# A planned instruction order with longer assumed latencies, four PSUM banks for first products, and three strided units in place of two

## Chip, cores and metric

The kernel runs on one core of a Trainium2 chip. The metric is device time in microseconds (us) for one launch, a median over runs.

## What is computed

Attention with 8 heads of 64 over 8 batches of 576 tokens. Four heads are local (a query sees the 32 tokens that end with it), four are strided (a query sees the earlier tokens with the same residue modulo 32). The result, 4608 tokens of 512 numbers, goes through an FF layer with a SoLU activation and a layer norm between its two weights.

```python
mask_local = (rel >= 0) & (rel < stride)
mask_strided = (rel >= 0) & (pos[None, :] % stride == pos[:, None] % stride)
...
attn = np.exp(scores)
attn = attn / (np.sum(attn, axis=-1, keepdims=True) + 1e-09)
...
h = x @ w_in
h_max = np.max(h, axis=-1, keepdims=True)
e = np.exp(h - h_max)
sm = e / (np.sum(e, axis=-1, keepdims=True) + 1e-09)
solu = h * sm
...
ln = (solu - mu) / np.sqrt(var + 1e-06) * g_ln
return (ln @ w_out).astype(np.float32)
```

## The kernel before

**Attention units.** A batch is cut into units: two strided ones of 6 and 5 blocks (a block is 3 residues of 18 tokens, 54 queries against 54 keys) and three local ones of 3 blocks (64 queries against 96 keys). A unit's steps are: scores into s_ps on PE (L341 adds the mask, L346 multiplies), max and subtraction on DVE (L352, L353), exp on ACT (L355), sum and reciprocal on DVE (L356, L360, L361), scaling on POOL (L364), a high half in fp16 on ACT (L370) and the low half on DVE (L371), a transpose by DMA from p to pt (L373), second products into x_ps on PE (L394), and high and low half of x on ACT (L410) and DVE (L411) into the rings xhi and xlo. x_ps has two banks: local units take them in turn, a strided unit takes both.

**FF tiles.** There are 36 tiles of 128 tokens. Tile n: first products in two halves of 12 matmuls each into h_ps (L452 to L454, a half is 512 columns, one bank), the max on DVE (L459) and its scaling (L460), exp on ACT (L461), u = h times e on DVE (L463), its square sum on ACT (L467), small steps on POOL (L471 to L487), c in a high half on ACT (L484) and a low half on DVE (L485), a transpose by DMA from c to ct (L488), second products into o_ps in two halves of 12 matmuls (L492 to L494), and a scaled copy with the store on ACT (L500, L501). h_ps has three banks, and tile n takes the pairs (0, 1), (0, 2), (1, 2) in turn. The last tile takes x_ps for its first products, and the last two tiles take s_ps for their second.

**Preparation.** Weights come as 64-bit numbers that are decoded on ACT and DVE, scaled, and split into fp16 halves; V is scaled and split for every batch (L301, L302) and copied to other partitions by DMA (L317: ve for local, vd for strided units). All loads, moves and transposes are issued by SP, in one queue; only the output's stores are issued by ACT.

**The order.** Nothing is issued where it is written: every step is added to a `Plan` with an engine, a duration, a key (its due time, in the same unit for all engines) and the buffers that it reads and writes. `Plan.order` is a list schedule: at each point it takes, of the steps that are ready on an engine, the one with the lowest key, and its model says when the steps behind it are ready. A transfer ends `DMA_LATENCY` after its queue time, and a step on another engine is ready `HOP` after the one that it needs. The order that comes out is the order in which each engine gets its instructions; the times of the model go nowhere. The keys are UK for units (one unit per 1.0 of time), TK for tiles (1.11 apart).

In the plan a bank of h_ps or x_ps is a buffer of its own, `("h", i)` and `("x", i)`. The tensors themselves are one tile each, and the waits of the built program are set by the framework from the order.

Of the kernel before, what the change touches and what calls it, by code (L numbers as in the profile page):

```python
# [25 lines left out]
KL = QL + STRIDE  # L26
# [3 lines left out]

RS = 3
QS = RS * NI
R0 = {0: 0, 6: STRIDE - 5 * RS}
RES = [*range(6 * RS), *range(STRIDE - 5 * RS, STRIDE)]
SP = len(RES) * NI

UNITS = [(1, 0, 6), (1, 6, 5), (0, 0, 3), (0, 3, 3), (0, 6, 3)]
NU = len(UNITS)
P_SCALE = 64.0
EPS_SM = 1e-9  # L40
# [5 lines left out]

UK = [-40.0, -39.5, -39.0, -8.0, -7.0, *(n - 6.0 for n in range(5, B * NU))]
TK = [1.11 * t + 1.0 for t in range(NT)]  # L50
G2LAG = 0.55
KX = 0.5
# [8 lines left out]
class Plan:  # L61
# [6 lines left out]
    def __init__(self):  # L70
        self.steps = []
# [68 lines left out]
def attn_solu_kernel(ctx: ExitStack, tc: tile.TileContext, qloc, qstr, kloc, kstr, vloc, vstr, w_in, w_out, g, masks, out):  # L140
    nc = tc.nc
    sb = ctx.enter_context(tc.tile_pool(name="sb", bufs=1))
    ps = ctx.enter_context(tc.tile_pool(name="ps", bufs=1, space=PSUM))


    NTB, NPB, NPT, NCB, NCT = 4, 3, 2, 2, 3

    def buf(name, shape, dtype=F32, n=1):
        return [sb.tile(shape, dtype, name=f"{name}{i}") for i in range(n)]


# [12 lines left out]

    (mask_sb,) = buf("mask", [P, 3, KL])
    (mk_loc,) = buf("mk_loc", [P, 2, 3, KL], BF16)
    (mk_str,) = buf("mk_str", [P, 6, QS], BF16)
    (unit_sb,) = buf("unit", [P, P], BF16)
    t_sb = buf("t", [P, 12 * QS], n=NTB)
    m_sb = buf("m", [P, 24], n=NTB + 1)  # L170
    p_sb = buf("p", [P, 12, P], F16, n=NPB)
    pt_sb = buf("pt", [P, 12, P], F16, n=NPT)
# [23 lines left out]
    (gs_sb,) = buf("gs", [P, 8])  # L196

    s_ps = ps.tile([P, 2, 512], F32, name="s_ps")
    h_ps = ps.tile([P, 3, 512], F32, name="h_ps")
    x_ps = ps.tile([P, 2, 512], F32, name="x_ps")  # L200
    o_ps = ps.tile([P, DM], F32, name="o_ps")

    plan = Plan()
    add = plan.add
# [7 lines left out]
    def masks_bf16():  # L212
        m = mask_sb
        nc.vector.tensor_copy(mk_loc[:, 0, 0:1], m[:, 0:1])
        nc.vector.tensor_copy(mk_loc[:, 0, 1:3], m[:, 1:2].broadcast_to([P, 2, KL]))
        nc.vector.tensor_copy(mk_loc[:, 1], m[:, 1:2].broadcast_to([P, 3, KL]))
        nc.vector.tensor_copy(mk_str, m[:, 2:3, 0:QS].broadcast_to([P, 6, QS]))

    def load_masks(key):
        add("sp", 0.6, lambda: nc.sync.dma_start(mask_sb, masks), key, w=["mask_raw"])  # L220
# [47 lines left out]
    def load_qk(b, half, key):  # L268
        w = 2 * (S, SP)[half]
        k0 = 0 if half else KPAD  # L270
# [45 lines left out]
        for i, (dur, dst, src) in enumerate(moves):  # L316
            add("sp", dur, lambda dst=dst, src=src: nc.sync.dma_start(dst, src), key, r=[("v", a, 0), ("v", a, 1)], w=[("v2", a, i)])  # L317

    plan_x = [0]


    def unit(n, key):
        b, j = divmod(n, NU)
        half, b0, nb = UNITS[j]
        nq, nk = (QL, KL) if half == 0 else (QS, QS)
        nx = 2 * nb
        t, m, pb, ptb = t_sb[n % NTB], m_sb[n % (NTB + 1)], p_sb[n % NPB], pt_sb[n % NPT]
# [23 lines left out]
        w = nx * nk / 960  # L351
# [19 lines left out]
        add("dve", w + 0.1, lambda: nc.vector.tensor_tensor(lo, tv, hi, op=ALU.subtract), key + 0.45, r=[T, PB], w=[PB], lock=True)  # L371
        nt = nx if half else 2 * nx
        add("sp", 0.16 * nt, lambda: nc.sync.dma_start_transpose(ptb[:, 0:nt], pb[:, 0:nt].rearrange("p a k -> p (a k)")), key + 0.5, r=[PB], w=[PT])  # L373
        xb = plan_x[0] % 2
        if half == 0:
            plan_x[0] += 1
        X = [("x", xb)] if half == 0 else [("x", 0), ("x", 1)]

        def pv():
            for pair in range(2):  # L380
                for i in range(nb):
                    blk, x = b0 + i, pair * nb + i
# [28 lines left out]
        add("dve", nx * nq / 960 + 0.15, lambda: nc.vector.tensor_tensor(dl, src, dh, op=ALU.subtract), key + KX, r=[*X, *((*x, "h") for x in ring)],  # L411
            w=[(*x, "l") for x in ring])


    def ff(n, key):

        banks, halves = (((0, 1), (0, 1)), ((0, 2), (1, 0)), ((1, 2), (0, 1)))[n % 3]
        hv, o, O = h_ps[:, banks[0] : banks[1] + 1 : banks[1] - banks[0]], o_ps, "o"
        HH = [("h", i) for i in banks]

        if n >= NT - 2:
            o, O = s_ps[:, n % 2], ("s", n % 2)
        if n == NT - 1:
            hv, HH = x_ps, [("x", i) for i in range(2)]
# [4 lines left out]
        ring += [("xs", b % 2, b0, a) for b in bs for b0 in R0 for a in "hl"]  # L429
# [26 lines left out]
        for i in halves:  # L456
# [11 lines left out]
            r=[U, (ST, "mean")], w=[E, (ST, "sq")])  # L468
# [8 lines left out]
        def norms():  # L477
# [8 lines left out]
            r=[U, (ST, "r"), (C, 0)], w=[(C, 1)], lock=True)  # L486
# [182 lines left out]
```

## Time and profile before

| | us |
|---|---|
| median of 3 runs | 612.12 |
| lowest and highest | 610.24, 617.36 |
| the profiled execution | 613.98 |
| its span, first to last instruction | 612.3 |
| PE, DVE, ACT, POOL busy in the span | 496.2, 368.5, 297.6, 153.7 |
| mean granted clock of TensorE | 0.946 |

The profile is of one execution. Busy times of engines overlap, so they don't add up to the span. A matmul's duration in the rows (0.38 us) is longer than the distance to the next one (0.22 us), since matmuls are pipelined. A wait names the instruction that waited, then the one that released it.

### The profile page before, as it was taken

To read this page: it belongs to the slowest core of one execution; us is meant where nothing else is said; L and a number is where in the kernel's file an instruction comes from. 1 tells how busy PE (TensorE), PEld (TensorE's weight loads), DVE (VectorE), ACT (ScalarE), POOL (GpSimd) and SP (SyncE) were. 2 spreads that over 40 slices of the span, in tenths; PEclk is the share of its full clock that TensorE was granted. 3 is DMA by queue.
4 is the path that set the end of the run, shared out by engine and by line. 5 is a ranking of instruction groups with operands and counts; after the bars stand their busy time and mean duration, and the time that the engine had idled before them with its cause. 6 is when DMAs were issued, how large, how long until landed. Compare 5 with 4: busy or idle time off the path is not lost.

```text
span 612.3 us, 11764 instructions
## 1 busy us (share of the span) xinstructions
PE 496.2 (81%) x4808; PEld 254.8 (42%) x4808; DVE 368.5 (60%) x647; ACT 297.6 (49%) x437; POOL 153.7 (25%) x305
## 2 busy tenths in 40 slices
PE   0236925879987899899998999789998889899865
PEld 0233523435444454435454444434454444344322
DVE  3578888866567557666574667476665664333340
ACT  3746536545643565346543464356534453333440
POOL 2020004333222323223322132244222232113130
PEclk9999965989989999879998899799999998999979
DMA  8799587789529983988378847974497554422252
GB/s 320 292 241 280 149 155 206 179 179 233 99 55 205 247 216 78 204 212 201 79 164 199 212 95 171 216 194 114 100 211 125 108 97 82 85 53 52 51 112 59
DMA packets 171157, 96.89 MB, mean 158 GB/s; under 512 B 138208, under 2 KB 157280, under 8 KB 171104
## 3 DMA queue, kind: packets, MB, share of 16 engines
q1 hardware_dynamic: 165920, 86.71, 63.1%
q10 hardware_dynamic: 5184, 9.44, 4.9%
q8 instruction: 37, 0.61, 0.4%
q14 instruction: 16, 0.13, 0.1%
HBM read 39.24 MB, written 9.44 MB: 80 GB/s over the span
## 4 chain that ended last, share of the span: by engine, by line
PE 36%; DVE 23%; ACT 13%; DMA 12%; POOL 8%; issue 7%; ACTq 1%; SPq 0%; DVEq 0%; POOLq 0%
PE h_ps L452 7%; PE h_ps L454 6%; PE h_ps L453 6%; DVE u L463 4%; DMA pt<-p 4%; DVE st L459 4%; PE o_ps L492 4%; ACT e L461 4%; PE o_ps L494 4%; PE o_ps L493 4%; DMA ct<-c 3%; DMA vrl<-vloc 3%; POOL t L364 3%; DVE c L485 2%; PE x_ps L394 2%
## 5 line engine op out<-in xcount | busy, mean ns | idle before, releaser
L452 PE MATMUL h_ps<-w,xhi 128*128 128x512 f16 x280 | 112.5, 402 | 30.3 <-DVE st L459 14.3
L492 PE MATMUL o_ps<-obuf,ct 128*128 128x512 f16 x272 | 104.2, 383 | 11.4 <-DMA ct<-c 11.4
L453 PE MATMUL h_ps<-w,xhi 128*128 128x512 f16 x280 | 112.6, 402 | 0.0
L454 PE MATMUL h_ps<-w,xlo 128*128 128x512 f16 x280 | 112.4, 401 | 0.0
L493 PE MATMUL o_ps<-obuf,ct 128*128 128x512 f16 x272 | 104.0, 382 | 0.0
L494 PE MATMUL o_ps<-obuf,ct 128*128 128x512 f16 x272 | 103.9, 382 | 0.0
L461 ACT ACTIVATE e<-h_ps,st,vsc 128x1024 f32<-128x1024 f32 x31 | 37.3, 1204 | 109.5 <-PE h_ps L454 57.8
L471 POOL TENSOR_SCALAR st<-st 128x1 f32<-128x1 f32 x36 | 10.3, 286 | 293.1 <-DVE st L466 287.7
L364 POOL TENSOR_TENSOR t<-t,m 128x576 f32<-128x576 f32 (+2 forms) x40 | 52.5, 1314 | 122.6 <-DVE m L361 95.9
L463 DVE SCALAR_TENSOR_TENSOR u<-h_ps,e 128x1024 f32<-128x1024 f32 x35 | 42.8, 1222 | 64.0 <-ACT e L461 49.8
L485 DVE SCALAR_TENSOR_TENSOR c<-u,st,c 128x1024 f16<-128x1024 f32 x36 | 47.3, 1315 | 39.9 <-ACT c L484 39.9
L459 DVE TENSOR_REDUCE st<-h_ps 128x1 f32<-128x1024 f32 x35 | 42.5, 1216 | 32.2 <-PE h_ps L454 32.2
L467 ACT ACTIVATE e<-u,st 128x1024 f32<-128x1024 f32 x36 | 41.3, 1147 | 40.8 <-DVE st L466 40.8
L453 PEld LDWEIGHTS <-xhi 128*128 128x128 f16 x288 | 29.3, 102 | 63.1 <-issue 37.4
L484 ACT ACTIVATE c<-u,st 128x1024 f16<-128x1024 f32 x36 | 41.2, 1146 | 26.2 <-POOL st L481 25.3
L492 PEld LDWEIGHTS <-ct 128*128 128x128 f16 x288 | 28.4, 99 | 51.9 <-DMA ct<-c 19.2
L371 DVE TENSOR_TENSOR p<-t,p 128x576 f16<-128x576 f32 (+2 forms) x40 | 30.5, 762 | 26.1 <-ACT p L370 25.8
L454 PEld LDWEIGHTS <-xlo 128*128 128x128 f16 x288 | 29.5, 102 | 38.0 <-issue 7.1
L452 PEld LDWEIGHTS <-xhi 128*128 128x128 f16 x288 | 29.6, 103 | 35.2 <-issue 6.7
L494 PEld LDWEIGHTS <-ct 128*128 128x128 f16 x288 | 28.4, 99 | 34.6 <-issue 1.1
L346 PE MATMUL s_ps<-k,q 64*54 64x54 f32 (+1 forms) x1280 | 41.9, 275 | 0.0
L493 PEld LDWEIGHTS <-ct 128*128 128x128 f16 x288 | 28.4, 98 | 32.0 <-issue 0.8
(125 smaller groups left out, 730.0 us busy)
## 6 DMA issues: line engine op xcount, KB each, us to landing
out<-ob ACTq DMA_DIRECT2D x36, 256.0 KB, 3.4
vrs<-vstr SPq DMA_DIRECT2D x8, 768.0 KB, 6.9
vd<-vs SPq DMA_DIRECT2D x16, 384.0 KB, 5.9
vrl<-vloc SPq DMA_DIRECT2D x8, 640.0 KB, 6.2
q<-qstr SPq DMA_DIRECT2D x8, 594.0 KB, 4.9
k<-kstr SPq DMA_DIRECT2D x8, 594.0 KB, 6.0
q<-qloc SPq DMA_DIRECT2D x8, 576.0 KB, 6.2
k<-kloc SPq DMA_DIRECT2D x8, 576.0 KB, 5.9
```

The costliest lines, as they stand in the source:

```text
L346: nc.tensor.matmul(s_ps[row : row + nq, pair, i * nk : (i + 1) * nk], q_raw[half][hs, q0 : q0 + (nq - 1) * nqb + 1 : nqb], k_raw[half][hs, ...
L364: add("pool", nx * nk / 500 + 0.1, lambda: nc.gpsimd.tensor_tensor(tv, tv, sm.unsqueeze(2).broadcast_to([P, nx, nk]), op=ALU.mult), key + ...
L452: nc.tensor.matmul(hv[:, i], xhi[:, cc, tok], whi[:, cc, cols], start=(cc == 0), stop=False)
L453: nc.tensor.matmul(hv[:, i], xhi[:, cc, tok], wlo[:, cc, cols], start=False, stop=False)
L454: nc.tensor.matmul(hv[:, i], xlo[:, cc, tok], whi[:, cc, cols], start=False, stop=(cc == 3))
L459: add("dve", 1.21, lambda: nc.vector.tensor_reduce(nm, hv, axis=AX.XY, op=ALU.max, negate=True), key + 0.2, r=HH, w=[(ST, "nm")])
L461: add("act", 1.3, lambda: nc.scalar.activation(ev, hv, AF.Exp, bias=nm, scale=hs, accum_out=z), key + 0.25, r=[*HH, (ST, "nm"), *SC], w=[E ...
L463: add("dve", 1.3, lambda: nc.vector.scalar_tensor_tensor(uv, hv, 1.0, ev, op0=ALU.mult, op1=ALU.mult, accum_out=us), key + 0.3, r=[*HH, E] ...
L485: add("dve", 1.35, lambda: nc.vector.scalar_tensor_tensor(c[:, 1], u, r, c[:, 0], op0=ALU.mult, op1=ALU.subtract), key + 0.45, r=[U, (ST, ...
L492: nc.tensor.matmul(o, ct[:, cc, :], ohi[:, cc, :], start=(cc == 0), stop=False)
L493: nc.tensor.matmul(o, ct[:, cc, :], olo[:, cc, :], start=False, stop=False)
L494: nc.tensor.matmul(o, ct[:, 8 + cc, :], ohi[:, cc, :], start=False, stop=(cc == 7))
```

## The change

It changes the cost model of the plan, the sizes of the strided units, and the use of PSUM.

- `DMA_LATENCY` goes from 2.0 to 6.0 and `HOP` from 0.1 to 0.6.
- The strided half of a batch becomes three units of 4, 4 and 3 blocks. The second of them holds residues 12 to 17 and again 17 to 22 (residue 17 is computed twice, as before), so its copies into xhi and xlo are two instructions each. UK is stretched so that a batch takes the same time in keys.
- h_ps gets four banks, tile n takes the pair 0, 1 or 2, 3 in turn, the last tile too. x_ps has one bank, which every unit takes.

```diff
-UNITS = [(1, 0, 6), (1, 6, 5), (0, 0, 3), (0, 3, 3), (0, 6, 3)]
+NBS = SP // QS
+
+UNITS = [(1, 0, 4), (1, 4, 4), (1, 8, 3), (0, 0, 3), (0, 3, 3), (0, 6, 3)]
...
-UK = [-40.0, -39.5, -39.0, -8.0, -7.0, *(n - 6.0 for n in range(5, B * NU))]
+UK = [-40.0, -39.7, -39.4, -39.0, -8.0, -7.0, *(5 / 6 * n - 6.0 for n in range(NU, B * NU))]
...
-    DMA_LATENCY = 2.0
+    DMA_LATENCY = 6.0
     DMA_AHEAD = 1.0
-    HOP = 0.1
+    HOP = 0.6
...
-    h_ps = ps.tile([P, 3, 512], F32, name="h_ps")
-    x_ps = ps.tile([P, 2, 512], F32, name="x_ps")
+    h_ps = ps.tile([P, 4, 512], F32, name="h_ps")
+    x_ps = ps.tile([P, 512], F32, name="x_ps")
...
-        X = [("x", xb)] if half == 0 else [("x", 0), ("x", 1)]
+        X = ["x"]
...
+            res = RES[RS * b0 : RS * (b0 + nb)]
+            cuts = [0, *(i for i in range(1, len(res)) if res[i] != res[i - 1] + 1), len(res)]
+            parts = [(src[:, :, :, i:j], *(x[:, :, :, res[i] : res[i] + j - i] for x in to)) for i, j in zip(cuts, cuts[1:])]
...
-        banks, halves = (((0, 1), (0, 1)), ((0, 2), (1, 0)), ((1, 2), (0, 1)))[n % 3]
-        hv, o, O = h_ps[:, banks[0] : banks[1] + 1 : banks[1] - banks[0]], o_ps, "o"
-        HH = [("h", i) for i in banks]
+        h0 = n % 2 * 2
+        hv, o, O = h_ps[:, h0 : h0 + 2], o_ps, "o"
+        HH = [("h", h0 + i) for i in range(2)]
...
-        if n == NT - 1:
-            hv, HH = x_ps, [("x", i) for i in range(2)]
...
-        for j in range(2):
+        for j in range(3):
             unit(b * NU + j, UK[b * NU + j])
```

The order of every engine moves with it, and the line numbers of the unit's and the tile's steps by two to three. Three places follow; the numbers in the names are buffers and tell tiles and units apart.

SP in batch 2, from the transpose of the second strided unit's p on, before. ct1 and ct2 are the transposed c of tiles 4 and 5, pt0 holds the first local unit, vd is V for the strided units of batch 3:

```order
L373 DMA_TRANSPOSE pt1_101<-p2_99 128x10x128
L373 DMA_TRANSPOSE pt0_100<-p0_97 128x12x128
L488 DMA_TRANSPOSE ct1_111<-c0_108 128x16x128
L317 DMA vd0_77<-vs0_75 64x12x256 x2
L488 DMA_TRANSPOSE ct2_112<-c1_109 128x16x128
L271 DMA q00_63<-qloc 128x1152
L272 DMA k00_65<-kloc 128x1152
L373 DMA_TRANSPOSE pt1_101<-p1_98 128x12x128
L317 DMA vd0_77<-vs0_75 64x6x256 x2
```

and now, from the transpose of the third strided unit's p on:

```order
L371 DMA_TRANSPOSE pt0_100<-p2_99 128x6x128
L490 DMA_TRANSPOSE ct1_111<-c0_108 128x16x128
L371 DMA_TRANSPOSE pt1_101<-p0_97 128x12x128
L490 DMA_TRANSPOSE ct2_112<-c1_109 128x16x128
L271 DMA q00_63<-qloc 128x1152
L272 DMA k00_65<-kloc 128x1152
L317 DMA vd0_77<-vs0_75 64x12x256 x2
L317 DMA vd0_77<-vs0_75 64x6x256 x2
L371 DMA_TRANSPOSE pt0_100<-p1_98 128x12x128
```

The moves of vd, which wait for the split of V, stood between the two tiles' transposes and behind the next unit's, and now stand together behind the loads.

DVE from the max of tile 11 to its u, before (L459 max, L460 scaling, L463 u; L352, L353 and L371 belong to units, L411 is the low half of x):

```order
L459 TENSOR_REDUCE st3_118<-h_ps_130 128x1
L460 TENSOR_SCALAR st3_118<-st3_118,vsc2_82 128x1
L352 TENSOR_REDUCE m0_92<-s_ps_129 128x12
L411 TENSOR_TENSOR xlo0_103<-x_ps_131,xhi0_102 128x2x192
L371 TENSOR_TENSOR p1_98<-t3_91,p1_98 128x6x96
L353 TENSOR_TENSOR t0_88<-s_ps_129,m0_92 128x648
L463 SCALAR_TENSOR_TENSOR u1_107,st3_118<-h_ps_130,e1_105 128x1024
```

and now, between the same three of tile 11 (now L461, L462 and L465; the other lines have moved by two or three as well):

```order
L461 TENSOR_REDUCE st3_118<-h_ps_130 128x1
L302 SCALAR_TENSOR_TENSOR vs0_75<-vrs0_73,vsc0_80,vs0_75 128x1536
L350 TENSOR_REDUCE m3_95<-s_ps_129 128x6
L369 TENSOR_TENSOR p1_98<-t2_90,p1_98 128x6x96
L351 TENSOR_TENSOR t3_91<-s_ps_129,m3_95 128x576
L487 SCALAR_TENSOR_TENSOR c0_108<-u0_106,st2_117,c0_108 128x1024
L462 TENSOR_SCALAR st3_118<-st3_118,vsc2_82 128x1
L414 TENSOR_TENSOR xlo0_103<-x_ps_131,xhi0_102 128x2x192
L354 TENSOR_REDUCE m3_95<-t3_91 128x6
L358 TENSOR_SCALAR m3_95<-m3_95 128x6
L359 RECIPROCAL m3_95<-m3_95 128x6
L465 SCALAR_TENSOR_TENSOR u1_107,st3_118<-h_ps_130,e1_105 128x1024
```

The scaling, which exp needs, stood right behind the max and now stands behind the split of V, three steps of units and the low half of tile 10's c.

ACT over the last tiles, before (L461 exp, L467 square sum, L484 c, L500 the scaled copy of the second products; st0 to st3 are tiles 32 to 35):

```order
L461 ACTIVATE e1_105,st1_116<-h_ps_130,st1_116,vsc3_83 128x1024
L467 ACTIVATE e1_105,st1_116<-u1_107,st1_116 128x1024
L461 ACTIVATE e1_105,st3_118<-x_ps_131,st3_118,vsc3_83 128x1024
L484 ACTIVATE c1_109<-u1_107,st1_116 128x1024
L500 ACTIVATE ob0_113<-o_ps_132,st0_115 128x512
L501 DMA out<-ob0_113 128x512
L461 ACTIVATE e0_104,st2_117<-h_ps_130,st2_117,vsc3_83 128x1024
L467 ACTIVATE e1_105,st3_118<-u1_107,st3_118 128x1024
L467 ACTIVATE e0_104,st2_117<-u0_106,st2_117 128x1024
L484 ACTIVATE c1_109<-u1_107,st3_118 128x1024
L484 ACTIVATE c0_108<-u0_106,st2_117 128x1024
L500 ACTIVATE ob1_114<-o_ps_132,st1_116 128x512
```

and now:

```order
L463 ACTIVATE e1_105,st1_116<-h_ps_130,st1_116,vsc3_83 128x1024
L469 ACTIVATE e1_105,st1_116<-u1_107,st1_116 128x1024
L463 ACTIVATE e0_104,st2_117<-h_ps_130,st2_117,vsc3_83 128x1024
L502 ACTIVATE ob1_114<-o_ps_132,st3_118 128x512
L503 DMA out<-ob1_114 128x512
L486 ACTIVATE c1_109<-u1_107,st1_116 128x1024
L469 ACTIVATE e0_104,st2_117<-u0_106,st2_117 128x1024
L486 ACTIVATE c0_108<-u0_106,st2_117 128x1024
L463 ACTIVATE e1_105,st3_118<-h_ps_130,st3_118,vsc3_83 128x1024
L502 ACTIVATE ob0_113<-o_ps_132,st0_115 128x512
L503 DMA out<-ob0_113 128x512
L469 ACTIVATE e1_105,st3_118<-u1_107,st3_118 128x1024
```

Tile 35 stood ahead of tile 34, with x_ps for its first products; now the tiles stand in turn, and the scaled copy of tile 32's second products comes behind the exp of tile 35 instead of ahead of tile 34's. On PE the second products of tiles 32 to 35 now stand behind the last first product.

## Rows read from the trace of the kernel before

**Rows 1.** The page: the engines' line of part 1 and the chain of part 4.

```profile
PE 496.2 (81%) x4808; PEld 254.8 (42%) x4808; DVE 368.5 (60%) x647; ACT 297.6 (49%) x437; POOL 153.7 (25%) x305
...
PE 36%; DVE 23%; ACT 13%; DMA 12%; POOL 8%; issue 7%; ACTq 1%; SPq 0%; DVEq 0%; POOLq 0%
```

**Rows 2.** Three stretches: length, busy us by engine, then PEclk, DMA share, GB/s.

```profile
0.00:100.00 100.00, 40.62 (x604) 28.19 (x608) 73.32 (x142) 52.28 (x85) 13.19 (x20) 0.91 0.87 246
100.00:580.00 480.00, 436.22 (x4136) 218.98 (x4129) 287.32 (x495) 236.46 (x341) 134.53 (x271) 0.96 0.67 145
580.00:612.00 32.00, 19.40 (x78) 7.65 (x75) 7.88 (x11) 8.84 (x13) 5.96 (x14) 0.88 0.35 82
```

**Rows 3.** Waits of PE from 100 to 580 us: total us, times, longest.

```profile
PE h_ps L452 <- DVE st L459: 14.3, 13, 2.6
PE h_ps L452 <- DVE u L463: 9.0, 9, 1.4
PE x_ps L394 <- DMA pt<-p: 7.4, 7, 2.5
PE h_ps L452 <- ACT e L461: 6.7, 4, 1.8
PE o_ps L492 <- DMA ct<-c: 6.3, 6, 2.3
```

**Rows 4.** Waits of PE: the longest before 100 us, and those behind 580 us.

```profile
PE s_ps L341 <- DVE t L353: 21.6, 7, 5.2
...
PE o_ps L492 <- DMA ct<-c: 5.0, 1, 5.0
PE s_ps L492 <- DMA ct<-c: 2.8, 2, 1.5
```

**Rows 5.** Timeline, 176 to 200 us: tile 6's reads and tile 7's first half.

```profile
184.90 1.21 DVE L459 TENSOR_REDUCE st<-h_ps 128x1 f32<-128x1024 f32 x1
...
186.16 0.38 PE L452 MATMUL h_ps<-w,xhi 128*128 128x512 f16 x1 [1.91 <-DVE st L459]
...
188.95 1.21 ACT L461 ACTIVATE e<-h_ps,st,vsc 128x1024 f32<-128x1024 f32 x1 [6.16 <-PE h_ps L454]
...
190.28 1.22 DVE L463 SCALAR_TENSOR_TENSOR u<-h_ps,e 128x1024 f32<-128x1024 f32 x1 [2.46 <-ACT e L461]
```

**Rows 6.** Waits of ACT (first row) and of DVE from 100 to 580 us.

```profile
ACT e L461 <- PE h_ps L454: 57.8, 13, 7.9
...
DVE u L463 <- ACT e L461: 48.4, 22, 4.8
DVE st L459 <- PE h_ps L454: 32.2, 13, 3.9
```

**Rows 7.** The transposed tiles pt (first row) and ct: from issue to landing.

```profile
DMA to landing us min/median/max: 3.4/4.3/8.6
...
DMA to landing us min/median/max: 4.2/5.0/8.4
```

**Rows 8.** Timeline, 570 to 612 us: tile 33's max and its second products.

```profile
572.03 1.23 DVE L459 TENSOR_REDUCE st<-h_ps 128x1 f32<-128x1024 f32 x1 [3.30 <-PE h_ps L454]
...
586.17 0.61 PE L492 MATMUL o_ps<-obuf,ct 128*128 128x512 f16 x1 [5.04 <-DMA ct<-c]
```

**Rows 9.** Groups of instructions by line and shape: count, busy us, mean ns, idle before.

```profile
L353 DVE TENSOR_TENSOR t<-s_ps,m 128x648 f32<-128x648 f32 x8 | 6.6, 828 | 0.2
...
L353 DVE TENSOR_TENSOR t<-s_ps,m 128x540 f32<-128x540 f32 x8 | 5.8, 719 | 0.2
...
L361 DVE RECIPROCAL m<-m 128x10 f32<-128x10 f32 x8 | 1.7, 217 | 0.3
```

**Rows 10.** Timeline of PE, 200 to 270 us: the scores of one strided unit.

```profile
214.30 0.31 PE L341 MATMUL s_ps<-mk_str,unit 64*64 64x270 bf16 x4
214.44 1.15 PE L346 MATMUL s_ps<-k,q 64*54 64x54 f32 x40
```

More of the change, by code (lines that the diff above doesn't have):

```diff
@@ L32 @@
 QS = RS * NI
-R0 = {0: 0, 6: STRIDE - 5 * RS}
 RES = [*range(6 * RS), *range(STRIDE - 5 * RS, STRIDE)]
 SP = len(RES) * NI
-UNITS = [(1, 0, 6), (1, 6, 5), (0, 0, 3), (0, 3, 3), (0, 6, 3)]
+NBS = SP // QS
+UNITS = [(1, 0, 4), (1, 4, 4), (1, 8, 3), (0, 0, 3), (0, 3, 3), (0, 6, 3)]
 NU = len(UNITS)
@@ L166, in attn_solu_kernel @@
     (mk_loc,) = buf("mk_loc", [P, 2, 3, KL], BF16)
-    (mk_str,) = buf("mk_str", [P, 6, QS], BF16)
+    (mk_str,) = buf("mk_str", [P, 4, QS], BF16)
     (unit_sb,) = buf("unit", [P, P], BF16)
-    t_sb = buf("t", [P, 12 * QS], n=NTB)
+    t_sb = buf("t", [P, 6 * KL], n=NTB)
     m_sb = buf("m", [P, 24], n=NTB + 1)
@@ L216, in masks_bf16 @@
         nc.vector.tensor_copy(mk_loc[:, 1], m[:, 1:2].broadcast_to([P, 3, KL]))
-        nc.vector.tensor_copy(mk_str, m[:, 2:3, 0:QS].broadcast_to([P, 6, QS]))
+        nc.vector.tensor_copy(mk_str, m[:, 2:3, 0:QS].broadcast_to([P, 4, QS]))
     def load_masks(key):
@@ L317, in v_split @@
             add("sp", dur, lambda dst=dst, src=src: nc.sync.dma_start(dst, src), key, r=[("v", a, 0), ("v", a, 1)], w=[("v2", a, i)])
-    plan_x = [0]
     def unit(n, key):
@@ L373, in unit @@
         add("sp", 0.16 * nt, lambda: nc.sync.dma_start_transpose(ptb[:, 0:nt], pb[:, 0:nt].rearrange("p a k -> p (a k)")), key + 0.5, r=[PB], w=[PT])
-        xb = plan_x[0] % 2
-        if half == 0:
-            plan_x[0] += 1
-        X = [("x", xb)] if half == 0 else [("x", 0), ("x", 1)]
+        X = ["x"]
         def pv():
@@ L382, in pv @@
                     blk, x = b0 + i, pair * nb + i
+                    x_out = x_ps[:, x * nq :]
                     if half == 0:
-                        x_out = x_ps[:, xb, x * nq :]
                         vv, vb = (v_sb[0] if blk % 2 else ve_sb), (blk + 1) // 2
@@ L387, in pv @@
                     else:
-                        x_out = x_ps[:, pair, i * nq :]
                         vv, vb = vd_sb.rearrange("p a c y d -> p a (c y d)"), blk
@@ L401, in unit @@
             q0, w = off + QL * b0, QL * nb
-            src = x_ps[:, xb, 0 : 2 * w].rearrange("p (c q) -> p c q", c=2)
-            dh, dl = (x[:, 0:2, q0 : q0 + w] for x in (xhi, xlo))
+            src = x_ps[:, 0 : 2 * w].rearrange("p (c q) -> p c q", c=2)
+            parts = [(src, *(x[:, 0:2, q0 : q0 + w] for x in (xhi, xlo)))]
             ring = [("xl", q0 // QL + i) for i in range(nb)]
         else:
-            src = x_ps[:, :, 0 : nb * QS].rearrange("p c (r i) -> p c i r", i=NI)
-            dh, dl = (x[:, 2:4, off : off + S].rearrange("p c (i r) -> p c i r", r=STRIDE)[:, :, :, R0[b0] : R0[b0] + RS * nb] for x in (xhi, xlo))
@@ L409, in unit @@
-            ring = [("xs", b % 2, b0)]
-        add("act", nx * nq / 1200 + 0.17, lambda: nc.scalar.copy(dh, src), key + KX, r=X, w=[(*x, "h") for x in ring])
-        add("dve", nx * nq / 960 + 0.15, lambda: nc.vector.tensor_tensor(dl, src, dh, op=ALU.subtract), key + KX, r=[*X, *((*x, "h") for x in ring)],
-            w=[(*x, "l") for x in ring])
+            src = x_ps[:, 0 : nx * QS].rearrange("p (c r i) -> p c i r", c=2, i=NI)
+            to = [x[:, 2:4, off : off + S].rearrange("p c (i r) -> p c i r", r=STRIDE) for x in (xhi, xlo)]
@@ new lines, in unit, with x_hi, x_lo @@
+            res = RES[RS * b0 : RS * (b0 + nb)]
+            cuts = [0, *(i for i in range(1, len(res)) if res[i] != res[i - 1] + 1), len(res)]
+            parts = [(src[:, :, :, i:j], *(x[:, :, :, res[i] : res[i] + j - i] for x in to)) for i, j in zip(cuts, cuts[1:])]
+            ring = [("xs", b % 2, b0)]
+        def x_hi():
+            for src, dh, _ in parts:
+                nc.scalar.copy(dh, src)
+        def x_lo():
+            for src, dh, dl in parts:
+                nc.vector.tensor_tensor(dl, src, dh, op=ALU.subtract)
@@ L415, in ff @@
+        add("act", nx * nq / 1200 + 0.17 * len(parts), x_hi, key + KX, r=X, w=[(*x, "h") for x in ring])
+        add("dve", nx * nq / 960 + 0.15 * len(parts), x_lo, key + KX, r=[*X, *((*x, "h") for x in ring)], w=[(*x, "l") for x in ring])
     def ff(n, key):
-        banks, halves = (((0, 1), (0, 1)), ((0, 2), (1, 0)), ((1, 2), (0, 1)))[n % 3]
-        hv, o, O = h_ps[:, banks[0] : banks[1] + 1 : banks[1] - banks[0]], o_ps, "o"
-        HH = [("h", i) for i in banks]
+        h0 = n % 2 * 2
@@ L428, in ff @@
         ring = [("xl", pos // QL + i, a) for i in range(2) for a in "hl"]
-        ring += [("xs", b % 2, b0, a) for b in bs for b0 in R0 for a in "hl"]
+        ring += [("xs", b % 2, b0, a) for b in bs for half, b0, _ in UNITS if half for a in "hl"]
         e, u, c, ct, ob, st = e_sb[n % 2], u_sb[n % 2], c_sb[n % NCB], ct_sb[n % NCT], ob_sb[n % 2], st_sb[n % 4]
@@ L454, in g1 @@
                 nc.tensor.matmul(hv[:, i], xlo[:, cc, tok], whi[:, cc, cols], start=False, stop=(cc == 3))
-        for i in halves:
+        for i in range(2):
             add("pe", 2.6, lambda i=i: g1(i), key, r=[*ring, *(("w", cc) for cc in range(4))], w=[HH[i]])
@@ L594, in attn_solu_kernel @@
         v_split(b, 0, VK[b] + 2.5)
-        for j in range(2, NU - 1):
+        for j in range(3, NU - 1):
             unit(b * NU + j, UK[b * NU + j])
```

## The prediction

> **What bounds the kernel now.** I read the page's engine line and its chain first [rows 1]: TensorE (PE) is busy 81% of the span, but holds only 36% of the chain that ended last; VectorE (DVE), ScalarE (ACT), the transfers and POOL hold 23, 13, 12 and 8%. So PE has the most work, and still spends time waiting for a chain through the others. Then the stretches [rows 2]: in the first 100 us PE works 40.6 us, from 100 to 580 it works 436.2 of 480, in the last 32 it works 19.4. The middle is the run of token tiles; its idle time is 43.8 us.
>
> PE's waits in that middle [rows 3] add up to the same: 14.3 + 9.0 + 6.7 + 7.4 + 6.3 = 43.7. Of this 30.0 us stands before first products (L452), which wait for a read of h_ps; 7.4 before the attention's second products, which wait for a transposed p; 6.3 before the second products of the FF (L492), which wait for a transposed c. In the last stretch it is 5.0 + 2.8 us for c, and at the start the score matmuls wait 21.6 us for L353, the last DVE read of the scores [rows 4].
>
> The 30.0 us is not what the plan meant. In [rows 5] stand tile 6 (banks 0 and 1) and tile 7 (first half in bank 2). The first half of tile 7 (PE at 186.16) starts when the max of tile 6 (DVE at 184.90) has ended, 1.91 us late, though that max reads other banks. The exp of tile 6 (ACT at 188.95) has its max since 186.1, and starts only when that half has been written. In all, exp waited 57.8 us for first products and max 32.2 [rows 6]; how much of that is a tile's own products, the sums don't tell. I read it so: a write of h_ps and a read of h_ps exclude each other, in the order in which the steps are issued, whatever the bank.
>
> **The change, part by part.** The sum is made on the profiled execution: 613.98 us, of which 612.3 are its span; the median of the runs shown is 612.12, or 1.9 lower.
>
> *Transfers planned 6.0 instead of 2.0 us late.* With its own costs the plan before expects a p of 12 blocks after 0.55 + 1.92 + 2.0 = 4.5 us, and a c after 0.55 + 2.55 + 2.0 = 5.1. The trace has medians of 4.3 and 5.0, and largest ones of 8.6 and 8.4 [rows 7]. The new plan expects 8.5 and 9.1, the upper ends. An order holds no clock times, so a pessimistic plan costs PE nothing while other work stands in front of the late step; it puts more there. Between the scores of the first local unit of batch 2 and its second products PE had 5 half-steps of the FF (2.6 us each), now 8; between tile 5's last first product and its second products 6, now 9. On the SP queue, shown with the change, the vd moves no longer stand between two transposes of c. Of the 7.4 + 6.3 us I take 12; bounds 0 (what was late for one step is late for the next) and 13.7.
>
> The Trainium skill, "DMA: Bandwidth & Descriptors", section "Anatomy of one DMA — SWDGE (gpsimd) path", gives a DMA a fixed cost of about 2 us, on another issuing path than this. By it the old figure was right and this part would save nothing; the trace agrees at the median and not at the largest, and the largest are what PE waits for.
>
> *Hand-overs at 0.6 instead of 0.1 us, and four banks.* If reads and writes of h_ps still exclude each other, four banks free nothing by themselves. I went through both orders half by half and set the reads that stand ahead of a half (max 1.21, exp 1.21, u 1.22 [rows 5], and some 0.2 us behind each) against the PE work that stands there. From tile 4 to 33 that leaves 10 us of unavoidable wait before, and 10.5 now. The measured 30.0 is three times that, because the reads begin late: DVE waited 48.4 us for exp [rows 6]. A plan with longer hand-overs puts other work into such holes, so that later reads come sooner. But it also parts the reads of one tile: over tiles 4 to 30 there are 36 steps between a max and its scaling, where there were 9, and 78 between scaling and u, where there were 53; the DVE rows of tile 11, shown with the change, are the worst of it. I take -5 us; bounds -30 (all gone) and +30 (doubled).
>
> *The end.* Before, the last tile was started early, into x_ps, and its second products stood among those of the two tiles before, so PE met c three times with nothing else to do: 5.0 + 2.8 us. Now the order is plain, and the second products of tiles 32, 33 and 34, six half-steps or 15.5 us, stand between the last first product and tile 35's. Before, it took 14.1 us from the start of a max (572.03) to the second products that its c released (586.17) [rows 8]; this is now covered. New are two waits for h_ps: the max of tile 33 (1.2) and exp and u of tile 34 (2.7). Gain 7.8 - 3.9 = 3.9; bounds 0 and 7.8. The granted clock of this stretch is 0.88 [rows 2], so 12% of 32 us, 3.8, went to the lower level (1.2 GHz) after idle stretches; of this I count 2.
>
> *The clock in the run.* From 100 to 580 the mean granted clock is 0.96 [rows 2]: 19 us went to work at 1.2 GHz instead of 2.4. With some 40% of the run's idle time gone (17 of 43.8) I take 4 us; bounds 0 and 12.
>
> *Units of 4, 4 and 3 blocks.* The elements stay the same, the passes grow. From 828 against 719 ns at 648 and 540 elements [rows 9] the fixed part of a DVE pass is 828 - 648 x 109/108 = 174 ns; five such passes, the reciprocal's 0.22 and as much for the scaling ahead of it, and one more x_lo because the middle unit is cut in two: 0.87 + 0.44 + 0.17, some 1.4 us per batch. In the run DVE is busy 287 of 480 us [rows 2], which hides it; with that cover gone it would be 8 x 1.4 = 11 us. In the first 100 us DVE is waited for, and two batches stand there: +2.8. The extra mask matmuls cost PE 0.14 us (214.30 to 214.44) per unit [rows 10]: +1.1 for 8. ACT and POOL get a pass more on engines that are busy half the time; nothing.
>
> *One bank for x.* No second product waits for a read of x [rows 3]; in the built program each already waited for the last x_lo issued before, of either bank. So nothing in the run, and +1.1 at the start, where the first two strided units stand back to back on PE. The reads of the first tiles' h_ps stand closer there too: +1.9, by the same count as above. Bounds for both together 0 and 8.
>
> Sum: -12 - 5 - 3.9 - 2 - 4 + 2.8 + 1.1 + 1.1 + 1.9 = -20.0. From 613.98 that is 594.0, from the median 592.1. I say 593.
>
> **The rivals.**
> A, the pairs of banks part after all, and reads no longer hold the next tile's products. For it speaks the code, two pairs that never touch; against it [rows 5], where different banks did not help. Then another 20 of the 30.0 us and 8 of the clock go: 593 - 28 = 565.
>
> The Trainium skill, "PSUM — Partial Sum Buffer", section "Terms", forbids two engines only the same bank and quadrant at once; by that rule rival A is what the chip allows. The trace shows that this program orders more than that.
>
> B, no change: what the transfers no longer hold, the reads of h_ps do, since PE comes to them earlier. Then the -12, -5 and -4 fall away: 593 + 21 = 614, by the median's measure 613. For it: h_ps has 69% of the run's idle time.
>
> C, slower: the parted reads decide. The reads of a tile must be over before the half that is issued behind them, and there are (36 - 9) + (78 - 53) = 52 more steps inside them, of some 0.75 us each [rows 9]: 39 us. If PE has nothing left in front of two thirds, that is +26 in place of -5: 593 + 31 = 624. The gain is gone when L452's waits reach 30 + 15 = 45 us; over 51 it is slower by 1%. Against it: what was put between had to be done anyway, and stands nowhere else now.
>
> **How the numbers follow.** Forecast 0.62, with 578 to 604 as its own range; A 0.08; B 0.15; C 0.15. About 1% is what a measurement of this kernel can tell from no change (its three runs lie 1.2% apart). Nearly all of the forecast and A are faster by over 1%: 0.69. Same, from B and the near ends of the forecast and of C: 0.17. Slower: 0.14. The range leaves out most of A and the upper half of C: 568 to 618.
>
> **What would show it.** Right: from 100 us on PE's waits for p and c fall under 3 us in all; the wait of 5.0 us near the end is gone; first products still wait 18 to 35 us for reads of h_ps, and exp still waits for the next tile's half. Wrong: over 45 us (C) or under 8 (A) of these; waits for p and c that stay over 8; a first 100 us that grows by over 8.

## The result, and the profile after

The changed kernel takes 584.07 us, the median of 4 runs (582.03 to 585.01), against 611.18 for the kernel before on the same chip. The ratio is 0.9539, with a 95% interval of 0.946 to 0.9618: some 4.6% faster. The forecast was 593, with 578 to 604 as the likeliest case's own range. An execution that took over 1.5% longer than the fastest of its kernel counts as a slow one, and the times and ratios of the experiments leave it out. The profiled execution took 584.25 us with a span of 582.3 (before 613.98 and 612.3).

The page of the changed kernel, the engines' line and the chain, to be held against [rows 1]:

```profile
PE 489.1 (84%) x4840; PEld 251.6 (43%) x4840; DVE 369.2 (63%) x711; ACT 300.3 (52%) x469; POOL 156.1 (27%) x313
...
PE 64%; DVE 18%; DMA 6%; issue 5%; ACT 3%; POOL 2%; SPq 1%; ACTq 0%; DVEq 0%; POOLq 0%
```

PE now holds 64% of the chain that ended last instead of 36%, the transfers 6% instead of 12. The three stretches, cut for the shorter span (length, busy us of PE, PEld, DVE, ACT and POOL, then PEclk, DMA share, GB/s), against [rows 2]:

```profile
0.00:100.00 100.00, 48.00 (x636) 29.89 (x637) 76.31 (x158) 54.93 (x94) 13.39 (x24) 0.91 0.86 242
100.00:550.00 450.00, 417.01 (x4098) 211.32 (x4097) 284.85 (x543) 233.70 (x360) 136.76 (x276) 0.98 0.72 155
550.00:582.00 32.00, 24.10 (x110) 10.37 (x108) 7.99 (x11) 11.63 (x16) 5.94 (x14) 1.00 0.37 91
```

The idle time of PE is the length of a stretch less its busy time. In the first 100 us it falls from 59.4 to 52.0, in the run of tiles from 43.8 to 33.0, in the last 32 us from 12.6 to 7.9. That is 22.9 of the 30.0 us by which the span is shorter. The other 7.1 is PE's busy time, 496.2 before and 489.1 now, although the work has grown by 32 instructions: a smaller part of it runs at the lower clock. The 33.0 us of the run, by what PE waited for (total us, times, longest), where [rows 3] stood:

```profile
PE h_ps L454 <- ACT e L463: 9.8, 4, 4.1
PE h_ps L454 <- DVE u L465: 8.6, 6, 2.7
PE h_ps L454 <- DVE st L461: 6.8, 10, 1.3
PE s_ps L339 <- DVE vsc L254: 6.3, 4, 1.9
PE x_ps L388 <- DVE xlo L414: 1.1, 2, 0.8
PE x_ps L388 <- DMA pt<-p: 0.4, 1, 0.4
```

The transfers are nearly gone from it: 0.4 us for p, none for c, where there were 13.7. The reads of h_ps are still there with 25.2 us (30.0 before), and a wait for L254 has come, one short DVE step in scaling V. Behind 550 us first products wait another 2.7 us for u, and the second products 1.0 us for c in place of the 5.0 and 2.8 of [rows 4].

One place shows what a wait for h_ps looks like. The timeline of the changed kernel from 122 to 142 us (start, length, engine, instruction, in brackets the idle time before it and its releaser):

```profile
129.78 1.21 ACT L463 ACTIVATE e<-h_ps,st,vsc 128x1024 f32<-128x1024 f32 x1
...
131.13 0.59 PE L454 MATMUL h_ps<-w,xhi 128*128 128x512 f16 x1 [4.13 <-ACT e L463]
131.51 0.63 PE L455 MATMUL h_ps<-w,xhi 128*128 128x512 f16 x1
...
135.72 0.38 PE L456 MATMUL h_ps<-w,xlo 128*128 128x512 f16 x1
...
136.22 1.22 DVE L465 SCALAR_TENSOR_TENSOR u<-h_ps,e 128x1024 f32<-128x1024 f32 x1 [5.23 <-PE h_ps L456]
```

PE stands still for 4.13 us until the exp of one tile has read its pair of banks, although the half that it then writes lies in the other pair. After that pause the matmuls come 0.4 us apart, so the half takes 4.6 us from first start to last; DVE's u of the tile that exp has just read waits 5.23 us until that half of the next tile is written. It is the same as in [rows 5], with four banks: a read and a write of h_ps wait for each other whatever the bank, in the order of issue. This is called the lock below.

### The profile page after: what moved, and what is told of

Same layout as the page of the kernel before. It is cut to its first block, busy times and chain, and to the rows that moved or that the text cites. A ratio compares the mean times of both kernels' runs of the same rounds, so it can differ in the third digit from the quotient of the medians.

```text
span 582.3 us, 11970 instructions
## 1 busy us (share of the span) xinstructions
PE 489.1 (84%) x4840; PEld 251.6 (43%) x4840; DVE 369.2 (63%) x711; ACT 300.3 (52%) x469; POOL 156.1 (27%) x313
## 4 chain that ended last, share of the span: by engine, by line
PE 64%; DVE 18%; DMA 6%; issue 5%; ACT 3%; POOL 2%; SPq 1%; ACTq 0%; DVEq 0%; POOLq 0%
PE h_ps L454 11%; PE h_ps L456 10%; PE h_ps L455 10%; PE o_ps L494 7%; PE o_ps L496 7%; PE o_ps L495 7%; PE x_ps L388 3%; PE s_ps L344 3%; DVE st L461 3%; DVE u L465 3%; DMA vrs<-vstr 2%; DMA pt<-p 2%; DMA room<-w_out 2%; DVE c L487 1%; DVE p L369 1%
## 5 line engine op out<-in xcount | busy, mean ns | idle before, releaser
L465 DVE SCALAR_TENSOR_TENSOR u<-h_ps,e 128x1024 f32<-128x1024 f32 x36 | 44.0, 1222 | 67.9 <-PE h_ps L456 45.5
L463 ACT ACTIVATE e<-h_ps,st,vsc 128x1024 f32<-128x1024 f32 x32 | 38.5, 1203 | 69.5 <-PE h_ps L456 34.2
L461 DVE TENSOR_REDUCE st<-h_ps 128x1 f32<-128x1024 f32 x36 | 43.8, 1217 | 39.8 <-PE h_ps L456 33.7
L487 DVE SCALAR_TENSOR_TENSOR c<-u,st,c 128x1024 f16<-128x1024 f32 x36 | 46.0, 1278 | 9.5 <-ACT c L486 9.5
L414 DVE TENSOR_TENSOR xlo<-x_ps,xhi 128x384 f16<-128x384 f32 (+3 forms) x56 | 28.1, 502 | 33.4 <-ACT xhi L410 32.9
L344 PE MATMUL s_ps<-k,q 64*54 64x54 f32 (+1 forms) x1280 | 43.4, 274 | 0.0
```

Source lines behind the costliest of these rows:

```text
L344: nc.tensor.matmul(s_ps[row : row + nq, pair, i * nk : (i + 1) * nk], q_raw[half][hs, q0 : q0 + (nq - 1) * nqb + 1 : nqb], k_raw[half][hs, ...
L487: add("dve", 1.35, lambda: nc.vector.scalar_tensor_tensor(c[:, 1], u, r, c[:, 0], op0=ALU.mult, op1=ALU.subtract), key + 0.45, r=[U, (ST, ...
```

## The experiments

Each is timed against the kernel before on the same chip; on the chips used that kernel took 609 to 611 us. The theory was that waits are set on h_ps as a whole, that the two constants of the plan's model bring the gain, and that the new layout alone brings none. The rivals were that the four banks bring it, or one of the constants alone.

**The constants and the layout.** The kernel before with the transfer constant alone:

```diff
-    DMA_LATENCY = 2.0
+    DMA_LATENCY = 6.0
```

> The kernel before with DMA_LATENCY 6.0 alone (HOP 0.1, three banks of h_ps, strided units of 6 and 5). If the late transfers carry the change, the waits of PE for p and c, 26.0 us over the whole execution before, fall under 6 us and the time to 590 to 598 us. If the hand-overs or the banks carry it, those waits fall too, but the time stays within 1% of 611, because the waits turn up again in front of first products (30 us before, then over 40).

Measured: 594.25 us, ratio 0.9698 (0.9637 to 0.976). From 100 us on, PE's waits for p and c fall from 7.4 + 6.3 + 5.0 + 2.8 = 21.5 us to 3.9, and the reads of h_ps keep 28.0. The time falls by 17.1, the waits for transfers by 17.6: the first expectation's range. Its sum of 26.0 us for the whole execution was too low (9.8 us before 100 us make it 31.3); that falls to 6.9, not quite under 6.

The kernel before with the hand-over constant alone:

```diff
-    HOP = 0.1
+    HOP = 0.6
```

> The kernel before with HOP 0.6 alone. If the late transfers carry the change, this is within 1% of 611 us and PE still waits over 15 us for p and c. If the hand-overs carry it, 590 to 598 us with waits for h_ps under 25 us.

Measured: 610.62 us (606.97 to 614.13), ratio 0.9995 (0.9941 to 1.005), no change, as the first expectation has it. But the waits have moved. The largest from 100 us on, by what PE waited for:

```profile
PE h_ps L452 <- DVE u L463: 17.0, 10, 3.9
PE o_ps L492 <- DMA ct<-c: 13.0, 5, 5.0
PE s_ps L492 <- DMA ct<-c: 5.8, 2, 4.2
PE x_ps L394 <- DMA pt<-p: 4.0, 3, 2.4
PE h_ps L452 <- ACT e L461: 3.3, 2, 2.7
PE h_ps L452 <- DVE st L459: 2.8, 7, 0.4
```

The reads of h_ps have gone from 30.0 to 23.1, c from 14.1 to 18.8, and p from 7.4 to 4.0.

The kernel before with both constants, no new layout:

```diff
-    DMA_LATENCY = 2.0
+    DMA_LATENCY = 6.0
-    HOP = 0.1
+    HOP = 0.6
```

> The kernel before with both model constants changed and nothing else. If the plan carries the change and the new layout of PSUM and units adds nothing, 580 to 590 us, as the changed kernel (584). If the four banks are needed, 595 us or more, with waits for h_ps as before (30 us).

Measured: 558.26 us (557.38 to 559.11), ratio 0.9115 (0.906 to 0.917): 26 us below the changed kernel and below both ranges that were expected. The two constants are worth 53 us here, far more than 17 and 0. The waits from 100 us on show both kinds gone at once, 7.6 us for h_ps and 2.9 for c:

```profile
PE h_ps L452 <- DVE st L459: 4.7, 7, 1.1
PE s_ps L492 <- DMA ct<-c: 2.2, 1, 2.2
...
PE h_ps L452 <- DVE u L463: 1.5, 3, 0.5
PE h_ps L452 <- ACT e L461: 1.4, 2, 0.7
...
PE o_ps L492 <- DMA ct<-c: 0.7, 1, 0.7
```

The changed kernel with the old constants, that is the layout alone:

```diff
-    DMA_LATENCY = 6.0
+    DMA_LATENCY = 2.0
-    HOP = 0.6
+    HOP = 0.1
```

> The changed kernel with the old constants 2.0 and 0.1: four banks of h_ps, one of x_ps and units of 4, 4 and 3 alone. If reads and writes of h_ps exclude each other whatever the bank, 605 to 620 us with waits for h_ps of 25 to 45 us: the layout alone gains nothing. If the banks part, under 600 us with waits for h_ps under 15.

Measured: 628.12 us (623.43 to 630.76), ratio 1.0245 (1.0154 to 1.0335). The layout alone makes the kernel slower, by more than was expected. In its profiled execution (633.07 us), from 100 us on, p is late by 21.3 us in ten waits, and h_ps holds 28.1, within the 25 to 45 of the first expectation.

**Is it the tensor that locks?** The changed kernel with its order kept to the last step, but h_ps as two tensors of two banks:

```diff
-    h_ps = ps.tile([P, 4, 512], F32, name="h_ps")
+    h_ps = [ps.tile([P, 2, 512], F32, name=f"h_ps{i}") for i in range(2)]
...
-        hv, o, O = h_ps[:, h0 : h0 + 2], o_ps, "o"
+        hv, o, O = h_ps[n % 2], o_ps, "o"
...
```

Two uses of h_ps as scratch space in the preparation go to the first tensor.

> The changed kernel with the two pairs of banks of h_ps as two tensors of two banks each, order and everything else as they are. If it is the one tensor over both pairs that makes reads and writes wait for each other, waits of PE for h_ps fall from 27.9 to under 8 us, exp waits for the other tile's half no longer, and the time falls to 555 to 572 us. If the waits for h_ps are a tile's own reads, or PE waits for something else instead, 580 to 588 us.

Measured: 541.42 us (541.35 to 541.71), ratio 0.8917 (0.8843 to 0.8991), the fastest of all kernels here, 43 us under the changed one and under the range that was expected. Of the 43 us of the profiled executions, 35.2 are idle time of PE and 7.5 its busy time. PE's waits from 100 us to the end:

```profile
PE h_ps L454 <- ACT xhi L410: 2.9, 1, 2.9
PE s_ps L494 <- DMA ct<-c: 1.0, 1, 1.0
PE o_ps L494 <- ACT ob L502: 0.8, 1, 0.8
PE s_ps L339 <- DVE vsc L254: 0.5, 1, 0.5
```

No first product waits for a read of h_ps any more, and the wait for L254 falls with them, from 6.3 to 0.5 us. The same place as in the timeline above, now from 112 to 126 us:

```profile
120.75 1.21 ACT L463 ACTIVATE e<-h_ps,st,vsc 128x1024 f32<-128x1024 f32 x1
...
120.91 0.39 PE L454 MATMUL h_ps<-w,xhi 128*128 128x512 f16 x1 [2.93 <-ACT xhi L410]
...
122.09 1.23 DVE L465 SCALAR_TENSOR_TENSOR u<-h_ps,e 128x1024 f32<-128x1024 f32 x1
...
122.57 0.63 PE L456 MATMUL h_ps<-w,xlo 128*128 128x512 f16 x1
```

exp reads one pair while PE writes the other, and u follows exp within 1.4 us where it had taken 6.4. PE itself still waits 2.93 us here, for xhi, so at this place the lock was worth 1.2 of PE's 4.13 us. The waits of DVE between 100 and 540 us, and in the last row one of ACT, for the changed kernel:

```profile
DVE u L465 <- PE h_ps L456: 45.5, 10, 6.7
DVE st L461 <- PE h_ps L456: 33.2, 16, 6.0
...
ACT e L463 <- PE h_ps L456: 29.0, 10, 6.1
```

and with two tensors, where ACT has no such wait:

```profile
DVE st L461 <- PE h_ps L456: 32.1, 17, 6.0
...
DVE u L465 <- ACT e L463: 11.3, 13, 2.4
```

The max keeps 32.1 of its 33.2 us, so these are its own tile's products. The 45.5 us of u and the 29.0 of exp were all for the next tile's. The run keeps the full clock:

```profile
100.00:520.00 420.00, 415.74 (x4101) 210.99 (x4098) 288.41 (x547) 240.72 (x369) 137.76 (x281) 1.00 0.81 168
```

The same two tensors with the old constants:

```diff
-    DMA_LATENCY = 6.0
+    DMA_LATENCY = 2.0
-    HOP = 0.6
+    HOP = 0.1
```

> Two tensors for h_ps and the old constants 2.0 and 0.1. If the one tensor cost the old constants as much as the new ones, this is 20 to 35 us under the kernel with the new layout and the old constants, with the waits for p and c still over 15 us. If the waits for p and c take the place of those for h_ps, less than 10 us under it.

Measured: 594.44 us, ratio 0.9782 (0.9678 to 0.9885). p is late by 23.2 us and c by 7.4. That is 34 us under the layout with the old constants, in the range of the first expectation. So the constants are worth 53 us here too, and free banks don't replace them.

**Each constant in the new layout.** The changed kernel with the old transfer constant:

```diff
-    DMA_LATENCY = 6.0
+    DMA_LATENCY = 2.0
```

> The changed kernel with DMA_LATENCY back at 2.0, HOP 0.6. If the late transfers carry the change, 596 to 612 us with over 15 us of PE waits for p and c. If the hand-overs carry it, 580 to 590.

and with the old hand-over constant:

```diff
-    HOP = 0.6
+    HOP = 0.1
```

> The changed kernel with HOP back at 0.1, DMA_LATENCY 6.0. If the late transfers carry the change, 580 to 592 us with under 5 us of PE waits for p and c. If the hand-overs carry it, 598 us or more.

Measured: 589.99 us, ratio 0.9728 (0.9618 to 0.9837), and 599.53 us, ratio 0.987 (0.9784 to 0.9956). With the old transfer constant p and c hold PE for 12.8 us and reads of h_ps for 14.5; with the old hand-over constant it is 8.9 and 30.1. Both times are in the range of the second expectation, the hand-overs'. Against 584 the transfer constant is worth 6 us here and the hand-over 15; in the old layout, from 558, it is 52 (611 to 558) and 36 (594 to 558). With the other numbers:

| transfer, hand-over | old layout | new layout | new, two tensors |
|---|---|---|---|
| 2.0, 0.1 | 611 | 628 | 594 |
| 6.0, 0.1 | 594 | 600 | 559 |
| 2.0, 0.6 | 611 | 590 | not run |
| 6.0, 0.6 | 558 | 584 | 541 |

Going from the old layout to the new costs 17, costs 5, gains 21 and costs 26 us, row by row. Neither a constant nor the layout has a price of its own: each changes the order, and the order decides.

**Which part of the layout costs the 26 us?** The theory was the fourth bank: the plan takes the two pairs as free, and the program locks them together. The kernel with both constants in the old layout, and the strided units of 4, 4 and 3 blocks:

```diff
-UNITS = [(1, 0, 6), (1, 6, 5), (0, 0, 3), (0, 3, 3), (0, 6, 3)]
+UNITS = [(1, 0, 4), (1, 4, 4), (1, 8, 3), (0, 0, 3), (0, 3, 3), (0, 6, 3)]
...
-        X = [("x", xb)] if half == 0 else [("x", 0), ("x", 1)]
+        X = [("x", xb)]
```

The keys UK are those of the changed kernel, and every unit now takes one of the two x banks, in turn.

> The kernel before with both constants (6.0 and 0.6; alone 558.3 us) and, of the new layout, only the strided units of 4, 4 and 3 blocks; three banks for h_ps and two for x as before. Theory 1, what the new layout costs is that the plan takes the four banks of h_ps as two free pairs: the units are nearly free here, 555 to 566 us, and first products wait under 12 us for reads of h_ps from 100 us on. Theory 2, the units cost it (more passes on DVE and ScalarE, more hand-overs): 572 to 590 us.

The changed kernel, its h_ps with three banks that rotate as before (and so also one x bank):

```diff
-    h_ps = ps.tile([P, 4, 512], F32, name="h_ps")
+    h_ps = ps.tile([P, 3, 512], F32, name="h_ps")
...
-        h0 = n % 2 * 2
-        hv, o, O = h_ps[:, h0 : h0 + 2], o_ps, "o"
-        HH = [("h", h0 + i) for i in range(2)]
+        banks, halves = (((0, 1), (0, 1)), ((0, 2), (1, 0)), ((1, 2), (0, 1)))[n % 3]
+        hv, o, O = h_ps[:, banks[0] : banks[1] + 1 : banks[1] - banks[0]], o_ps, "o"
+        HH = [("h", i) for i in banks]
...
-        for i in range(2):
+        for i in halves:
```

> The changed kernel with everything of the new layout but the fourth bank: h_ps has three banks that rotate as before, so that the plan holds a tile's second half behind the reads of the tile before. Theory 1, the fourth bank costs it: 552 to 568 us, waits for reads of h_ps from 100 us on fall from 25 us to under 12. Theory 2, units of 4, 4 and 3 or the single x bank cost it: 575 to 595 us, and the waits for h_ps stay over 18 us. A middle value, near 570, would share the cost between them.

Measured: 573.09 us (572.26 to 574.53) and 579.75 us (577.98 to 583.27). From 558 the units cost 15, the single x bank (with the last tile's move out of x_ps) 7, the fourth bank the last 4. The theory falls: most of the cost is the units', taken in this sequence of steps; another sequence was not tried. From 100 us on, in the kernel with the units alone:

```profile
PE h_ps L457 <- DVE st L464: 7.2, 10, 2.1
PE s_ps L339 <- DVE t L351: 5.8, 2, 2.9
PE h_ps L457 <- DVE u L468: 3.3, 3, 1.2
PE x_ps L389 <- DVE xlo L415: 2.5, 1, 2.5
```

h_ps has 10.5 us (7.6 in the old layout), and new are waits for the units' own chain, L351, the subtraction on the scores, and L415, the low half of x. So first products wait under 12 us, as the theory said, and yet the time is that of its rival. With one x bank the wait for L415 grows to 5.9, and h_ps holds 13.3, between the two expectations, where it holds 27.9 with the fourth bank: that bank doubles these waits and costs 4 us. In the kernel with the units alone PE is busy 399.5 of the 420 us from 100 on, at a clock of 0.97, where without them it was 408.7 at 0.99.

The last test of the theory tells the plan the truth, and changes the order only:

```diff
-        HH = [("h", h0 + i) for i in range(2)]
+        HH = ["h"]
...
-            add("pe", 2.6, lambda i=i: g1(i), key, r=[*ring, *(("w", cc) for cc in range(4))], w=[HH[i]])
+            add("pe", 2.6, lambda i=i: g1(i), key, r=[*ring, *(("w", cc) for cc in range(4))], w=HH)
...
```

> The changed kernel, its four banks and its addresses, but the plan is told that h_ps is one buffer: both halves of a tile come behind all reads of the tile before, which is what the program does anyway. Only the order changes. Theory 1, the plan's wrong belief is the cost: PE's waits for reads of h_ps fall from 25 us to 5 to 15, and the time to 555 to 575 us. Rival, the exclusion itself costs it and the order is as good as it can be: 580 us or more, since the plan now has only one tile's first products between reads.

Measured: 643.18 us, ratio 1.0487 (1.0413 to 1.056), 59 us slower than the changed kernel and far from the 555 to 575 of the theory; the rival's 580 or more holds. PE's waits from 100 us on:

```profile
PE h_ps L454 <- DVE u L465: 36.8, 16, 4.2
PE s_ps L339 <- DVE t L351: 10.2, 9, 2.5
PE s_ps L494 <- DMA ct<-c: 8.3, 1, 8.3
PE x_ps L388 <- DVE xlo L414: 6.2, 7, 2.1
```

With one buffer the plan gives PE no first products until u of the tile before, and there isn't enough other work to stand in front of 16 of these chains. Here a plan that believes the pairs free makes the better order, even for a program that locks them.

**Does the hand-over constant pay only for the lock?** The two tensors with the old hand-over constant:

```diff
-    HOP = 0.6
+    HOP = 0.1
```

> The changed kernel with h_ps as two tensors (541.4 us), with the hand-over constant put back from 0.6 to 0.1 and the transfer constant left at 6.0. Theory 1, the longer hand-over pays because it leaves room for reads of h_ps that begin late and hold the next tile: with two tensors that is gone, so the time stays within 536 to 548 us. Theory 2, it pays for every hand-over between engines (scores, x, probabilities): 552 to 570 us, as the 15 us that it was worth with one tensor, with new waits of PE for s_ps or x_ps.

Measured: 558.64 us, ratio 0.9187 (0.912 to 0.9254): 17 us lost against 541, in the range of the second theory, so the constant doesn't pay for the lock alone. The place is not the one expected, scores or x: PE waits for c, 2.8 us in the run and 8.3 at the end (1.0 with the constant at 0.6), and the first 100 us hold 47.0 us of PE work where they held 51.0.

## Why the prediction was right

It forecast 593 and 584 came, in its likeliest case's range. The signs that it named are there, and the sum is nearly right; two of its groups of terms were far off, in opposite directions. That they nearly cancel is luck.

**Transfers, -12.** Right in mechanism, and in size where it can be seen alone: the waits for p and c from 100 us on fall from 21.5 to 0.4 + 1.0 = 1.4 us, in the run alone from 13.7 to 0.4. With this constant alone the time falls by 17.1; the prediction had 12 for the run, and the 3.9 of the end beside it. The rule of the Trainium skill, "DMA: Bandwidth & Descriptors", section "Anatomy of one DMA — SWDGE (gpsimd) path", a fixed cost of about 2 us, was weighed as speaking for the old figure. As a number for the plan of these transposes, which SP issues, it is not enough here: pt and ct land after 4.2 and 4.5 us in the median, up to 9.8 and 10.4.

**Hand-overs and banks, -5.** The direction was right in the changed kernel, 30.0 to 27.9 us with the end counted, or -2. The hand-over constant alone is worth 0 in the old layout; with the other constant beside it, it is worth 36 there and 15 in the new. The step that failed is the one that priced this constant and the transfers' as terms to be added: in the old layout 17 + 0 became 53.

**The pairs don't part.** Shown: with the same order, and only the tensor cut in two, u no longer waits for the next tile's half, and 43 us go. The reading of [rows 5] was right, and rival A described what this cut brings, though it was sized at 565 where 541 was measured. The Trainium skill, "PSUM — Partial Sum Buffer", section "Terms", forbids two engines only the same bank and quadrant at once; the run with two tensors agrees, since exp at 120.75 reads one pair while PE writes the other at 120.91. The lock is in the waits that the program was built with, on the whole tensor.

**The parted reads, rival C.** 27.9 us of waits for h_ps are far from its 45. More steps stand between max, exp and u, but the waits of u only change their name: for exp 48.4 us [rows 6] and for products 14.3 before, 62.7 in all, now 17.3 and 45.5, 62.8 in all.

**No change, rival B.** Nothing took the place of the transfers but the 6.3 us behind L254, which no step had named. One of its four stands in the timeline of the changed kernel from 240 to 248 us:

```profile
239.96 1.22 DVE L465 SCALAR_TENSOR_TENSOR u<-h_ps,e 128x1024 f32<-128x1024 f32 x1 [6.71 <-PE h_ps L456]
...
241.11 0.15 DVE L254 TENSOR_SCALAR vsc<-s_ps 128x1 int32<-128x1 int32 x1
...
241.32 0.32 PE L339 MATMUL s_ps<-mk_loc,unit 64*64 64x288 bf16 x4 [1.47 <-DVE vsc L254]
```

u, held 6.71 us by the next tile's half, stands on DVE ahead of L254, and the scores wait for that: the lock at one remove. With two tensors the four together fall from 6.3 to 0.5 us.

**The layout, +6.9 in four terms** (units +2.8 and +1.1, one x bank +1.1, the first tiles' reads +1.9). This failed as a sum: PE's idle time in the first 100 us, where nearly all of it was placed, fell by 7.4. The term of the transfers counted waits from 100 us on only; waits for p before 100 us went from 9.8 to 4.4 and those for obuf, the decoded output weights, from 5.9 to 3.4. And the layout's price was looked for in the wrong stage: with both constants given it is 26 us, of which the units make 15. Only 1.6 us of that is PE work lost in the first 100 us (46.0 us there, 47.6 without the new units). Most of it lies in waits inside the run that the prediction had called hidden, since DVE is busy 287 of 480 us, though it named 11 us for the case that this cover is gone. DVE's idle time covered the passes themselves, not the waits of PE for the unit that comes next: 5.8 us for L351, 2.5 for L415 and 2.9 more for h_ps, by the rows of that kernel. A slip of the sum is small beside this: 0.87 + 0.44 + 0.17 is 1.5 us a batch, not 1.4.

**The end, -3.9, and the clock, -2 and -4.** PE's idle time at the end fell by 4.7: 7.8 us of waits for c went down to 1.0, and the two new waits came as described, 2.7 us for u of tile 34 and 1.3 for the max of tile 33, at 539.77 us and so ahead of the stretch as cut above. The plain order of the last tiles is not the only reason for the gain. With both constants and the last tile still in x_ps these waits for c are 2.2 us, with the new layout and the old constants 5.3. The mean clock of the last stretch is 1.00 (0.88 before), of the run 0.98 (0.96 before); PE's busy time falls by 7.1 us in all, where 6 were counted.

So the sum of -20 against -27 measured hides that the constants were priced too small (-27, with the end and the clock counted to them, against -53) and the layout too (+7 against +26).

## What to carry to other kernels

Before giving a buffer more banks, look in the timeline whether a read of one bank waits for a write of another: then cut the tensor in two, which here gave 43 us with the order untouched. Try the upper end of the measured landings in a list schedule's model, together with a longer hand-over: 6.0 and 0.6 gave the lowest time of those run in each of the three layouts, while the longer hand-over alone moved PE's waits from h_ps to c and gained nothing. Price a change of order by running its parts in pairs: single parts here gave -17, 0 and +17 us, which add up to 0, and the whole gave -27.

## What was not expected of the hardware

A stall of PE can cost more than itself. Around the 4.13 us at 131.13, and in a stretch without such a stall, the windows of the changed kernel say (columns as above, the clock third from the end):

```profile
120.00:131.00 11.00, 7.00 (x99) 3.91 (x97) 9.64 (x18) 5.18 (x9) 3.30 (x7) 0.90 0.92 219
131.00:136.00 5.00, 4.87 (x13) 1.78 (x13) 0.00 (x0) 2.14 (x4) 0.34 (x1) 0.53 1.10 228
200.00:204.00 4.00, 3.68 (x58) 2.04 (x54) 3.93 (x7) 0.42 (x1) 0.83 (x1) 1.00 1.11 262
```

The half behind the stall ran at 0.53, close to the lower level of 1.2 GHz, its matmuls 0.43 us apart; at 201 us they come 0.21 apart. That half cost 4.1 us of waiting and some 2.2 of clock (11 distances of up to 0.43 us instead of 0.21). Not every stall does this: behind the 2.65 us at 109.52 in the same trace the matmuls come 0.22 apart at once. Nor did the lock alone bring it, since with two tensors the same half, behind a stall of 2.93 us, has matmuls 0.43 apart as well. In the kernel with one buffer PE is busy for 516.1 us against 481.6 with two tensors, for the same 4840 matmuls.

The transposes' longest landings grew (8.6 to 9.8 us for pt, 8.4 to 10.4 for ct) while PE's waits for them nearly vanished, so it is the place in the order that decides, not the length. What remains open is why the two constants pay so much more together than alone; which steps of the order bring it was not tried one by one.
